# A layernorm, FFT filter and GELU kernel: filter rows loaded without pads, 31 warm-up matmuls, contiguous remainder weights and a new written-out order

## The chip, the cores and the metric

The kernel runs on one core of one Trainium2 chip. The metric is the device time of one execution in microseconds. Before the change the median of three runs is 148.87 us (148.75 to 149.37).

## The reference

The input x is 2048 x 640 in bf16. It is normalized over its 640 columns. Two branches read the result xn: a Fourier filter (two-dimensional real FFT, multiplication by the complex weights w_r + i w_i of 2048 x 321, inverse FFT) and a two-layer network with a GELU (640 to 1536 to 640). The output is x plus both.

```python
def _A_ref(x, w_r, w_i):
    B, S, D = x.shape
    X = jnp.fft.rfft2(x.astype(jnp.float32), axes=(-2, -1))
    X = X * (w_r + 1j * w_i)
    return jnp.fft.irfft2(X, s=(S, D), axes=(-2, -1)).astype(jnp.bfloat16)

def _B_ref(x, w1, b1, w2, b2):
    h = _gelu(jnp.einsum("bsd,df->bsf", x, w1) + b1)
    return jnp.einsum("bsf,fd->bsd", h, w2) + b2

xn = _layernorm(x, axis=-1)
return x + _A_ref(xn, w_r, w_i) + _B_ref(xn, w1, b1, w2, b2)
```

## The kernel before

The 2048 rows lie on 128 partitions, 16 chunks (numbered 0 to 15) of 640 columns each. The work goes through these stages.

- **Normalization (VectorE).** Each chunk has two batch-norm statistics (L480), their aggregation (L482), a reciprocal root (L490 and L491, the latter on GpSimd) and the scaling (L510), which writes xn. Sums and differences of mirrored columns (L540, L544) prepare the Fourier branch.
- **Transposes.** Layer 1 needs xn transposed (xnT). For chunks 0 to 3 TensorE does it (L528, copies at L394 and L395); for chunks 4 to 15 a DMA transpose issued by SyncE (L519).
- **Layer 1 (TensorE, all matmuls at L383).** Blocks of chunks 0-1, 2-3, 4-7, 8-11 and 12-15, each with 12 tiles of 128 hidden features (L575 to L584 for the first, L605 for the others). Five matmuls make one tile; ScalarE applies the GELU (L593, L611). A block needs the transposes of all its chunks. The order on TensorE is: block 0-1, block 2-3, part of layer 2, most of block 8-11, block 4-7, block 12-15.
- **Fourier branch.** Matmuls with the table gtab (L550), evacuated into XV (L556); groups of two or three chunks with the table etab (L635, "bps"); 32x32 matmuls with mtab (L653, "cps", evacuated into Y at L660); the filter itself on VectorE, two multiplications per pair (L678) that read Y and the filter weights Wf, and a sum and a difference (L682); 32x32 matmuls with ntab (L687, "dps"), evacuated into U; DMA transposes of U back into XV (L703); groups of two or three chunks with the table getab (L726, "eps"), evacuated into yo (L730), and sums of mirrored columns (L734, L739).
- **Layer 2 and the end.** Layer 2 (L761) is summed with the last matmul of the Fourier branch (table htab, L777) in PSUM; VectorE adds the bias or what was kept (L780) and writes the result, which a DMA adds onto x in the output (L787, GpSimd) or writes (L784, SyncE). Before that, GpSimd copies x into the output in four transfers (L563), after all filter weights have landed.

A group of matmuls with etab or getab (the functions `width` and `five`, L615 to L623) has four matmuls per chunk over 128 rows and four over 32 rows, the remainders. The stationary operand comes from XV: with etab 128 neighbouring columns, with getab 128 columns 16 elements apart.

The filter weights Wf lie as 32 rows per partition, real and imaginary rows in turn, each padded from 321 to KP = 322 elements; the pads are set to zero at L407, and every filter load waits for that. Partitions with even numbers hold rising rows of the weights, those with odd numbers falling ones. `load_w` (L448) loads 16 rows for 16 partitions at a time: nine loads for w_r, nine for w_i, all on SyncE's queue, one semaphore for all (group "W").

TensorE begins with 39 + 8 matmuls on zeros (`idle`, L409 to L413, WARM at L293). Then the bias of layer 1 is turned into a column by 12 small matmuls (L464).

The order of the work on each engine is written out by hand in ORDER (L253): each word is the number of an operation, a letter for its engine (s SyncE, p TensorE, a ScalarE, d VectorE, g GpSimd) and the PSUM or buffer slots. `arrange` puts the operations into that order, `sync` finds the waits. The numbers that `load`, `mm_us` and the like give as costs served only to find the order; they do nothing in the kernel. Each engine works its list in order, and SyncE issues its DMAs in the order of its list.

Of the kernel before, what the change touches and what calls it, by code (L numbers as in the profile page):

```python
# [9 lines left out]
ACT = mybir.ActivationFunctionType  # L10
# [78 lines left out]
def mm_us(n):  # L89
    return max(n / 2400.0 + 0.0027, 0.0265)  # L90
# [6 lines left out]
def act_us(n, ptr=0):  # L97
    return 0.067 + n / 1200.0 + 0.078 * ptr
# [155 lines left out]
9s 2a 0d 4g 6g 125p:1 3g 11a 10s 8p:6 12s 13s 14s 15s 55d 54d 16s 1d 17s 56d 60d 57a 18s 58a 59d 121d:1 19s 61d 124p:1 20s 122p:0 52p:7 62d 21s 123d 126a 63d 64g 22s 279p:0 249p:6  # L254
53a 289p:2 269p:1 23s 239p:5 259p:3 240p 127d 250p 24s 280p 270p 290p 133d:0 260p 25s 128p:4 130p:7 281p 129d 26s 251p 131a 132d 291p 261p 242p 252p 27s 241p 272p 68d 292p 271p 28s
243p 282p 69d 283p 253p 29s 262p 65d 244p 273p 274p 30s 284p 66d 254p 255p 70d 263p 67d 293p 245p 71d 134d:1 264p 72g 285p 135d 275p 137d 276p 256p 141d:0 278a 294p 246p 286p 144d
258a 142p:4 136d 248a 145p:7 143d 265p 247a 295p 146d 287a 266p 296p 148d:0 257a 305p:5 77d 288a 311p:7 147d 268a 323p:4 306p 85d 267a 314p:6 307a 312p 89d 315p 277a 332p:5 93d
297a 324p 92d 320p:3 298a 302p:0 101d 313a 321p 325a 100d 333p 326p:7 322a 152d:0 94d 308p:4 90d 316a 327p 151d 138p:1 91d 328a 139p 97d 309p 334a 95d 317p:6 98d 96g 140a 329p:7
102d 99d 330p 103d 149d 299p:5 5g 104g 184d:0 318p 331a 303p 150d 300p 182d 319a 7g 154p:1 81d 304a 153p 183s 197d:1 573p:6 301a 195d 310a 574p 186d:0 155a 196s 590p:4 187d 84d
575p 74d 591p 76d 198s 82d 576p 73d 592p 191d:1 185s 78d 189d 577p 188d 190d 578p 75d 83d 200d:0 31s 593p 79d 199d 32s 80g 192p:1 86d 594p 579d 33s 193p 113d 595p 34s 87d 203d:1  # L260
88g 374p:6 35s 204d 156d:1 375p 596d 157s 386p:0 376a 116d 377p:4 158d 194a 201d 159s 404p:7 114d 171d:0 398p:5 202d 115d 169d 36s 405p 161d:0 206p:1 172s 108d 406a 205p 117d 387p
207a 109d 389p:7 160d 170s 401p:6 118d 164d:1 388a 119d 165d 378p 120g 106d 37s 402p 163d 110d 379a 162d 390p 38s 221d:1 403a 399p 105d 39s 166p:0 223d 400a 167p 107d 356p:4 224s
111d 225d:0 391a 112g 226d 357p 359p:7 227d:1 358a 40s 229d 347p:5 228d 168a 230d 222s 173d:0 348p 174d 360p 210d:0 41s 231p:0 177d:0 361a 335p:6 208d 42s 349a 178d 232p 175d 336p
211s 176d 234a 212d:0 344p:7 213d 337a 180p:3 215d:1 209s 179p 216d 233a 345p 214d 350p:6 217d 181d 346a 43s 218p:0 219p 44s 365p:7 220a 45s 351p 338p:4 46s 352a 446p:0,0 47s 48s
366p 448d 447a 49s 339p 428p:5 50s 51s 443p:0,1 429p 445a 444d 410p:6 340a 733d 411p 367a 461p:0 434p:4 462a:1 463d:0 435p 430a 464p:0 436a 416p:5 235g 465d 466a 417p 412a 236g
471d:0 449p:0,1 418a 472d 237g 425p:7 450a 468d:1 238g 422p:4 467d 451a 426p 423p 469d:0 353p:5 473d:1 424a 470d 485p:0 427a 431p:4 487d:1 486a:0 432p 474d 626p:6 433a 478p:0
380p:4 480d:0 479a:2 381p 475p:0 382a 354p 477d 476a 419p:4 355a 484s 420p 488p:0 413p:5 490a 489d 483s 414p 421a 495d:1 455p:0,0 415a 481s 496d 392p:4 457a 456d 482s 383p:5 492d:0
393p 384p 394a 491d 452p:0,1 385a 498d:0 494d:1 368p:4 453a 454d 369p 341p:5 370a 497d 493d 512p:0 371p:4 513a:1 514d:0 372p 499p:0 373a 342p 500d:2 501a:0 362p:4 343a 363p 509p:0
395p:5 511d 510a 396p 515d:1 502p:0 627p 503a 504d 628p 364a 520d:0 505s 458p:0,1 397a 519d 629p 459a 507s 460d 609p:4 610p 516d 506s 536p:0 521d:0 630p 538a:0 518d:1 611p 517d
508s 537a:1 522d 631p 533p:0 612p 535a 534d 613p 632d 526p:0 614p 543d:0 527a:1 662p:6 540d:1 528a:2 663p 544d 523p:0 664p 615d 524a 665p 546d:1 525a 530s 645p:4 539d 666p 545d  # L270
667p 529s 541d:0 542d 646p 668d 647p 531s 547p:0 698p:6 548d:0 532s 699p 549d:1 700p 648p 550p:0 701p 551a 552d 702p 554s 703p 649p 704d 650p 556s 440p:7 651d 441p 553s 437p:4 442a
407p:5 555s 408p 564p:6 565p 438p 566p 557p:0 567p 558d:1 559a 568p 439a 560d:0 569p 409a 561d 583p:0 562d:0 563d 681p:4 585a:0 584d 570p 682p 571d:7 619p:0 586d:0 572g 587d 683p
620a:1 589d:1 684p 621a 588d 685p 686p 655p:0 687d 622d:0 600p:6 657a:0 743d 601p 623d 656a 602p 636p:4 580p:0 616p:2 581d:6 637p 638p 617d:2 639p 625d:0 618g 603p 624d 640p 658d:0
652p:2 604p 653d:0 641p 654g 605p 606p 642p 607d:3 691p:0 643d:5 608g 672p:6 659d 693a:1 644g 673p 692a 633p:4 674p 660d:0 675p 634d:7 676p 661d 635g 726p:0 695d:0 708p:4 582g
727a:0 694d 677p 728a 709p 678p 597p:0 679d:2 669p:2 710p 598d:0 680g 711p 688p:6 670d:7 712p 599g 697d:1 713p 696d 734p:0 689d:4 717p:2 714p 718p 690g 715d:5 719p 729d:0 671g 735p
730d 753p:7 720p 716g 705p:4 736p 706d:2 737p 732d:0 707g 721p 731d 722p 723p 738p 724d:1 739p 725g 744p:4 745p 746p 740p 747p 741d:7 754p 755p 748p 756p 749p 742s 750p 757p 762p:6
751d:0 758p 759p 763p 764p 760d 752s 765p 766p 767p 761s 768p 769d 770s
# [15 lines left out]
WARM = (39, 8)  # L293
# [3 lines left out]
def bass_parallel_sum__spectral_gfnet__dense_activation_gelu__prompt_kernel(  # L297
# [21 lines left out]
    with ExitStack() as es:  # L319
# [93 lines left out]
        idle(WARM[0], 0.1067 * 32 + (WARM[0] - 32) * mm_us(128))  # L413

# [18 lines left out]
        for j, at in enumerate((5.92, 6.93, 7.9, 9.75, 10.7)):  # L433
            if j == 3:
                load_x(2, 2, next(pr), at=8.75)
            load(W1[:, F * j:F * j + F], w1v[:, j, :], B_w1s[j], 393216, prio=next(pr), at=at)
        load(gtab[:], const["G"], B_g, 524288, prio=next(pr), at=12.0)
        for c, at in zip(range(4, 16, 2), (13.2, 14.7, 15.5, 16.3, 17.1, 17.9)):
            load_x(c, 2, next(pr), at=at)
# [8 lines left out]
        def load_w(wsrc, p0, off, row, n, step):  # L448
            w_ops.append(load(bass.AP(tensor=Wf, offset=p0 * WP + off, ap=[[2 * WP, 16], [2 * KP, n], [1, 321]]),
                 bass.AP(tensor=wsrc.tensor, offset=wsrc.offset + row * 321, ap=[[128 * 321, 16], [step * 321, n], [1, 321]]),  # L450
                 B_w, 16 * 642 * n, after=[wpad], rate=150e3, issue=0.645, group="W", prio=next(pr)))
        for ri, wsrc in enumerate((A_w_r, A_w_i)):
            for half in range(4):
                p0, off = 32 * half, ri * KP
                load_w(wsrc, p0, off, 16 * half, 16, 1)
                if half:
                    load_w(wsrc, p0 + 1, off, 128 - 16 * half, 16, -1)
                else:
                    load_w(wsrc, p0 + 1, off, 64, 1, 1)
                    load_w(wsrc, p0 + 1, off + 2 * KP, 127, 15, -1)  # L460
# [3 lines left out]
        pe([("128", 0.7)], 200, lambda: [(psb(B_b1ps.slot, [[1, 1]], fc), part(gT, 0, 1, 512 * (fc // 4) + fc % 4, [[4, 128]]), ident[0:1, 0:1], True, True)  # L464
# [30 lines left out]
        for pair in range(8):  # L495
# [10 lines left out]
            for n in range(2):  # L506
# [15 lines left out]
                for j0, j1, engs in ((0, 2, ["dve"]), (2, 5, ["act"])) if c < 2 else ((0, 5, ["dve", "act"]),):  # L522
# [7 lines left out]
                    tp = K.op([("pe", nj * mm_us(128))], pr, xt, reads=[B_xn, xn, B_id], writes=[tps], segs=[("128", nj * mm_us(128))])  # L530
                    if j0 and not c:
                        idle(WARM[1], WARM[1] * mm_us(128), gate=[tp])
# [113 lines left out]
        for P in range(4):  # L646
# [20 lines left out]
            def wv(pair, r):  # L667
                return view(Wf, (16 * (pair % 2) + 4 * (pair // 2) + r) * KP, [[2 * KP, 2], [0, 2], [1, KP]])
# [53 lines left out]
        for gi, (c0, n) in enumerate(GROUPS):  # L722
# [3 lines left out]
            pe(five_segs(n, 0.045), pr, lambda c0=c0, n=n, eps_=eps_: five(  # L726
                eps_.slot, n, lambda i, g, p0, k: part(XV, p0, k, 2048 * g + c0 + i, [[16, 128]]), getab),
                reads=B_v + [B_ge], writes=[eps_], gate=[fin_ops[c0 - 5]] if c0 > 8 else [])
# [92 lines left out]
```

## Time and profile before

| | before |
|---|---|
| median of 3 runs | 148.87 us |
| the profiled execution | 149.58 us |
| its span, first to last instruction | 147.8 us |
| TensorE busy | 141.9 us (96%) |
| VectorE busy | 110.0 us (74%) |
| ScalarE busy | 72.3 us (49%) |
| multiplications by the filter, L678 | 16 of 822 ns |
| DMA transposes of xnT (L519), issue to landing | 2.5 / 3.6 / 5.0 us (least, median, most) |
| filter loads, issued between | 28.6 and 51.5 us |

The page lists per engine the busy time, then the span in 40 slices, the DMA queues, the chain of work that ended last (followed back from the last instruction to what released each step), the costliest groups of instructions, and the DMAs. "L383 PE MATMUL ps<-xnT,W" is a matmul of line 383 that writes the tile ps from xnT and W1; "<-" behind an idle time names what ended it. "SPq" is SyncE's queue, where a DMA is issued; "PEld" is TensorE's loading of weights. Matmul records can be missing.

### The profile page before, as it was taken

How to read it: one execution, taken by the hardware profiler on the slowest of the kernel's cores; microseconds unless marked ns; L12 is line 12 of the kernel's file. 1: busy time of each engine (PE TensorE's matmuls, PEld its weight loads, DVE VectorE, ACT ScalarE, POOL GpSimd, SP SyncE). 2: the span in 40 equal slices, each digit the busy share in tenths (PEclk: the TensorE clock that was granted, in tenths of full speed). 3: DMA queues.
4: the chain of work that ended last, by engine and by line, in shares of the span. 5: the costliest groups of instructions: out<-in, count | busy, mean ns of one | idle time of the engine just before them, and what ended most of it. 6: DMA issues, size and time to landing. Idle time of an engine off the chain costs nothing.

```text
span 147.8 us, 3951 instructions
## 1 busy us (share of the span) xinstructions
PE 141.9 (96%) x1677; PEld 90.5 (61%) x1692; DVE 110.0 (74%) x240; ACT 72.3 (49%) x118; POOL 21.5 (15%) x35
## 2 busy tenths in 40 slices
PE   7999999999799999999999999999999999999993
PEld 7999995655456645445644545555666656655573
DVE  2688999999996367856966979864099787769543
ACT  3615995047598579977775756121075400430000
POOL 1002040301200005000000000000002024545620
DMA  5999999569999998988700670475302107777974
GB/s 119 305 402 399 378 388 132 113 141 135 165 163 160 158 161 218 350 334 45 141 4 0 41 138 10 89 93 106 71 4 24 20 4 84 93 89 91 114 87 114
DMA packets 29843, 21.01 MB, mean 142 GB/s; under 512 B 20225, under 2 KB 27137, under 8 KB 29826
## 3 DMA queue, kind: packets, MB, share of 16 engines
q1 hardware_dynamic: 27232, 15.84, 49.7%
q0 software_dynamic: 2592, 4.92, 17.8%
q8 instruction: 13, 0.21, 0.6%
q14 instruction: 4, 0.03, 0.1%
q10 hardware_dynamic: 2, 0.00, 0.0%
HBM read 13.54 MB, written 5.24 MB: 127 GB/s over the span
## 4 chain that ended last, share of the span: by engine, by line
PE 89%; DVE 5%; DMA 2%; issue 2%; SPq 1%
PE ps L383 88%; DMA xnT<-T 2%; DVE W L780 1%; DVE stats L480 1%; PE ps L528 1%; DVE T L544 1%; DVE T L510 1%; DVE T L540 1%; DVE X L771 1%; SPq L519 1%; DVE mv L482 0%; DVE warm L399 0%; DVE ve L490 0%
## 5 line engine op out<-in xcount | busy, mean ns | idle before, releaser
L383 PE MATMUL ps<-xnT,W 128*128 128x512 bf16 (+2 forms) x336 | 56.9, 320 | 1.0 <-DMA xnT<-T 1.0
L383 PE MATMUL ps<-W,gT 128*128 128x128 bf16 (+3 forms) x382 | 55.0, 292 | 1.5 <-issue 1.0
L383 PEld LDWEIGHTS ps<-W,gT 128*128 128x128 bf16 x396 | 30.1, 98 | 22.5 <-issue 1.7
L383 PEld LDWEIGHTS ps<-xnT,W 128*128 128x128 bf16 x336 | 31.4, 114 | 18.5 <-ACT gT L611 2.8
L611 ACT ACTIVATE gT<-ps,b1col 128x512 bf16<-128x512 f32 (+1 forms) x48 | 28.4, 638 | 15.1 <-PE ps L383 15.1
L787 POOL DMA_DIRECT2D out_dram<-W x14 | 12.3, 990 | 71.0 <-DVE W L780 71.0
L394 ACT ACTIVATE Wf<-ps 128x960 bf16<-128x960 f32 (+1 forms) x10 | 8.5, 888 | 17.9 <-PE ps L383 17.9
L480 DVE BATCH_NORM_STATS2 stats<-X 128x6 f32<-128x320 bf16 x32 | 14.0, 477 | 2.1 <-DMA X<-in_A_x_dram 2.1
L678 DVE TENSOR_TENSOR T<-Y,Wf 128x1288 bf16<-128x1288 bf16 x16 | 12.5, 822 | 0.0
L491 POOL TENSOR_TENSOR rstd<-ve,mhalf 128x2 f32<-128x2 f32 (+1 forms) x8 | 6.0, 744 | 31.9 <-DVE ve L490 31.8
L395 DVE CAST Y<-ps 128x644 bf16<-128x644 f32 x7 | 5.8, 829 | 5.4 <-PE ps L383 5.4
L394 ACT ACTIVATE Xb<-ps 128x960 bf16<-128x960 f32 (+1 forms) x7 | 8.0, 1166 | 3.4 <-PE ps L383 3.3
L544 DVE TENSOR_TENSOR T<-T 128x512 bf16<-128x512 bf16 (+1 forms) x32 | 9.0, 313 | 0.2
L394 ACT ACTIVATE XV<-ps 128x1280 bf16<-128x1280 f32 (+2 forms) x8 | 8.9, 1109 | 0.5 <-PE ps L383 0.5
L395 DVE CAST Xb<-ps 128x960 bf16<-128x960 f32 (+1 forms) x5 | 5.5, 1105 | 4.2 <-PE ps L383 4.2
L394 ACT ACTIVATE Y<-ps 128x644 bf16<-128x644 f32 x9 | 6.3, 708 | 4.1 <-PE ps L383 4.0
L510 DVE TENSOR_SCALAR T<-X,mv,rstd 128x640 bf16<-128x640 bf16 x16 | 6.9, 441 | 1.5 <-POOL rstd L491 1.0
L383 PE MATMUL ps<-getab,XV 32*128 32x160 bf16 (+1 forms) x128 | 7.5, 242 | 0.0
L540 DVE TENSOR_TENSOR T<-T 128x640 bf16<-128x640 bf16 x16 | 7.4, 480 | 0.1
L739 DVE TENSOR_TENSOR Wf<-Wf 128x960 bf16<-128x960 bf16 (+1 forms) x12 | 6.7, 596 | 0.9 <-PE ps L383 0.8
L780 DVE TENSOR_TENSOR W<-ps,b2bc 128x640 bf16<-128x640 f32 x6 | 4.8, 821 | 3.3 <-PE ps L383 3.3
L383 PE MATMUL ps<-etab,XV 32*128 32x160 bf16 (+1 forms) x128 | 7.2, 232 | 0.0
(53 smaller groups left out, 123.1 us busy)
## 6 DMA issues: line engine op xcount, KB each, us to landing
out_dram<-in_A_x_dram POOLq DMA_DIRECT2D x4, 640.0 KB, 7.3
X<-in_A_x_dram SPq DMA_DIRECT2D x7, 320.0 KB, 9.4
out_dram<-W POOLq DMA_DIRECT2D x14, 160.0 KB, 3.4
W<-in_B_w_dram SPq DMA_DIRECT2D x5, 384.0 KB, 5.8
W<-in_B_w_dram SPq DMA_DIRECT2D x3, 640.0 KB, 12.8
Wf<-in_A_w_r_dram SPq DMA_DIRECT2D x7, 160.5 KB, 3.9
Wf<-in_A_w_i_dram SPq DMA_DIRECT2D x7, 160.5 KB, 4.6
gtab<-c_G SPq DMA_DIRECT2D x1, 512.0 KB, 9.1
```

The source lines that it names most:

```text
L383: ins = e.matmul(o_, lhsT=lw, rhs=rh, start=st, stop=sp_, skip_group_check=True)
L394: return e.activation(dst(), src(), ACT.Copy, scale=scale)
L395: return e.tensor_copy(dst(), src())
L480: st_ops.append(K.op([("dve", 0.393)], pr, lambda e, _, c=c, h=h: e.bn_stats(stats[:, c, 6 * h:6 * h + 6], view(X, c * D + H2 * h, [[1, H2 ...
L510: o = K.op([("dve", 0.356)], pr, lambda e, _, c=c, n=n, xnv=xnv: e.tensor_scalar(out=xnv(n, 0, [[1, D]]), in0=view(X, c * D, [[1, D]]), sc ...
L540: K.op([("dve", 0.39)], pr, lambda e, _, k=k, op=op, xnv=xnv, x1v=x1v: e.tensor_tensor(out=x1v(H2 * k, [[D, 2], [1, H2]]), in0=xnv(0, 0, [ ...
L544: ring_ops.append(K.op([("dve", 0.333 if w == 128 else 0.136)], pr, lambda e, _, op=op, x1v=x1v, xfv=xfv, o_=o_, o0=o0, o1=o1, w=w: e.tens ...
L611: K.op([("act", act_us(128 * nt, 1) + 0.02)], pr + PRIO["gelu"], lambda e, _, c0=c0, nt=nt, fc=fc, hps=hps: e.activation(gT[:, fc, 128 * c ...
L678: filt_ops.append(K.op([("dve", 0.738)], pr, lambda e, _, k=k, Y=Y, TB=TB, pair=pair: e.tensor_tensor(out=view(TT, TB.slot * 8 * KP + k * ...
L739: K.op([("dve", 0.068 + n / 6)], pr + 3, lambda e, _, k=k, op=op, y2=y2, yf=yf, n=n: e.tensor_tensor(out=view(Wf, YF + yf.slot * 3 * D + ( ...
L780: K.op([("dve", dve_us(w))], 95, lambda e, _, os_=os_, fps=fps, o0=o0, w=w, xo=xo, base=base: e.tensor_tensor(out=view(W1, OST + os_.slot ...
L787: last.append(K.op([("pool", 0.9)], 450, lambda e, _, c=c, os_=os_: e.dma_start(ov[:, c, :], view(W1, OST + os_.slot * D, [[1, D]]), accum ...
```

## The change

1. **Filter without pads.** Wf holds 16 real rows and then 16 imaginary rows per partition, 321 elements each, with no pads; the memset covers one element behind the last row. The multiplications read 322 elements per row from rows 321 apart, the last of them the first of the next row (it meets a zero of Y).
2. **Fewer filter loads.** The rising rows of all 64 even partitions come in one load for w_r and one for w_i, each partition one piece of 16 x 321 elements. The falling rows stay in loads of 16 partitions. 12 loads instead of 18.
3. **Warm-up.** 31 matmuls on zeros instead of 39 + 8; the 12 bias matmuls now come right behind them, ahead of the first transposes.
4. **Remainder copies.** For the last four groups with getab ScalarE copies the remainder's part of XV into contiguous columns of the buffer T, and the remainder matmuls read their stationary operand from there. The first two groups stay as they were.
5. **A new ORDER** for all engines.

```diff
-WARM = (39, 8)
+WARM = 31
...
-        wpad = K.op([("pool", 0.2)], 447, lambda e, _: e.memset(view(Wf, KP - 1, [[KP, 32], [1, 1]]), 0.0), writes=[B_wpad])
+        wpad = K.op([("pool", 0.2)], 447, lambda e, _: e.memset(view(Wf, 32 * 321, [[1, 1]]), 0.0), writes=[B_wpad])
...
+            dst, src, more = [[321, n], [1, 321]], [[step * 321, n], [1, 321]], dict(rate=155e3, issue=0.645)
+            if step > 0:
+                dst, src, more = [[1, 321 * n]], [[1, 321 * n]], dict(rate=350e3, issue=0.5)
+            if quarters > 1:
+                dst, src = [[2 * WP, 16 * quarters]] + dst, [[16 * 321, quarters], [128 * 321, 16]] + src
+            else:
+                dst, src = [[2 * WP, 16]] + dst, [[128 * 321, 16]] + src
...
+            off = ri * 16 * 321
+            load_w(wsrc, 0, off, 0, 16, 1, 4)
+            for half in range(1, 4):
+                load_w(wsrc, 32 * half + 1, off, 128 - 16 * half, 16, -1)
+            load_w(wsrc, 1, off, 64, 1, 1)
+            load_w(wsrc, 1, off + 321, 127, 15, -1)
...
-                return view(Wf, (16 * (pair % 2) + 4 * (pair // 2) + r) * KP, [[2 * KP, 2], [0, 2], [1, KP]])
+                return view(Wf, (16 * r + 8 * (pair % 2) + 2 * (pair // 2)) * 321, [[321, 2], [0, 2], [1, KP]])
...
+            if gi > 1:
+                K.op([("act", act_us(128 * n) + 0.18 * n)], pr + 5, lambda e, _, c0=c0, n=n: e.activation(
+                    view(TT, 128 * c0, [[128, n], [1, 128]]), view(XV, 4 * 2048 + c0, [[1, n], [16, 128]]), ACT.Copy), reads=B_v, writes=[B_xr], after=filt_ops)
...
+                eps_.slot, n, lambda i, g, p0, k: part(TT, p0, k, 128 * (c0 + i), [[1, 128]]) if gi > 1 and g == 4 else part(XV, p0, k, 2048 * g + c0 + i, [[16, 128]]), getab),
+                reads=B_v + [B_ge, B_xr], writes=[eps_], gate=[fin_ops[c0 - 5]] if c0 > 8 else [])
```

What the new ORDER does on SyncE's queue, written with names (T4 is the transpose of chunk 4, Wr and Wi loads of real and imaginary weights):

```
before: ... w2 w2 w2 etab mtab T8 T10 T11 T9 ntab Wr Wr Wr Wr T4 T5 Wr T7 T6 Wr Wr Wr T15 Wr T14 Wi Wi T13 T12 Wi Wi Wi Wi Wi Wi Wi getab htab ...
after:  ... w2 w2 w2 T9 T10 T11 T8 etab mtab ntab Wr(rising) T4 T5 T7 T6 Wr Wr Wr Wr Wr Wi(rising) Wi Wi Wi Wi T15 T13 T12 T14 Wi getab htab ...
```

On TensorE the stages keep their sequence; within them the tiles are arranged anew. On ScalarE the four remainder copies stand around the copies of the second group with getab (yo): the first ahead of it, the other three behind it and ahead of the third group's.

More of the change, by code (lines that the diff above doesn't have):

```diff
@@ L412, in idle @@
             return pe([("128", us)], 300, lambda: [(psb(b.slot, [[1, 128]]), warm[:], warm[:], True, True) for _ in range(n)], reads=[B_warm], writes=[b], **kw)
-        idle(WARM[0], 0.1067 * 32 + (WARM[0] - 32) * mm_us(128))
+        idle(WARM, WARM * mm_us(128))
         B_b1t, B_b2b = Buf("b1t"), Buf("b2")
@@ L432, in bass_parallel_sum__spectral_gfnet__dense_activation_gelu__prompt_kernel @@
         load(part(gT, 0, 1, 0, [[1, F]]), b1v, B_b1t, 3072, q="act", prio=409, at=3.2)
-        for j, at in enumerate((5.92, 6.93, 7.9, 9.75, 10.7)):
+        for j, at in enumerate((6.05, 7.05, 8.0, 9.85, 10.8)):
             if j == 3:
-                load_x(2, 2, next(pr), at=8.75)
+                load_x(2, 2, next(pr), at=8.85)
             load(W1[:, F * j:F * j + F], w1v[:, j, :], B_w1s[j], 393216, prio=next(pr), at=at)
-        load(gtab[:], const["G"], B_g, 524288, prio=next(pr), at=12.0)
-        for c, at in zip(range(4, 16, 2), (13.2, 14.7, 15.5, 16.3, 17.1, 17.9)):
+        load(gtab[:], const["G"], B_g, 524288, prio=next(pr), at=12.3)
+        for c, at in zip(range(4, 16, 2), (13.7, 14.9, 15.7, 16.55, 17.35, 18.15)):
             load_x(c, 2, next(pr), at=at)
@@ L446, in bass_parallel_sum__spectral_gfnet__dense_activation_gelu__prompt_kernel, with load_w @@
         WP = 32 * KP
[L448 to L451, printed above, removed]
-        for ri, wsrc in enumerate((A_w_r, A_w_i)):
[L453 to L460, printed above, removed]
+        def load_w(wsrc, p0, off, row, n, step, quarters=1):
+            dst, src, more = [[321, n], [1, 321]], [[step * 321, n], [1, 321]], dict(rate=155e3, issue=0.645)
[5 more added lines that the diff above has]
+                dst, src = [[2 * WP, 16]] + dst, [[128 * 321, 16]] + src
+            w_ops.append(load(bass.AP(tensor=Wf, offset=p0 * WP + off, ap=dst), bass.AP(tensor=wsrc.tensor, offset=wsrc.offset + row * 321, ap=src),
+                 B_w, 16 * 642 * n * quarters, group="W", prio=next(pr), **more))
+        for ri, wsrc in enumerate((A_w_r, A_w_i)):
+            off = ri * 16 * 321
[4 more added lines that the diff above has]
+            load_w(wsrc, 1, off + 321, 127, 15, -1)
         load(getab[:], const["GE"], B_ge, 204800, prio=next(pr))
@@ L529, in xt @@
                         return ins
-                    tp = K.op([("pe", nj * mm_us(128))], pr, xt, reads=[B_xn, xn, B_id], writes=[tps], segs=[("128", nj * mm_us(128))])
-                    if j0 and not c:
-                        idle(WARM[1], WARM[1] * mm_us(128), gate=[tp])
+                    tp = K.op([("pe", nj * mm_us(128))], pr, xt, reads=[B_xn, xn, B_id], writes=[tps], hard=[b1op], segs=[("128", nj * mm_us(128))])
                     us = {"dve": 0.06 + 0.068 * nj, "act": act_us(128 * nj)}
@@ L725, in bass_parallel_sum__spectral_gfnet__dense_activation_gelu__prompt_kernel @@
             eps_ = Buf(f"eps{gi}", psum, 4, ZONE["eps"])
-            pe(five_segs(n, 0.045), pr, lambda c0=c0, n=n, eps_=eps_: five(
-                eps_.slot, n, lambda i, g, p0, k: part(XV, p0, k, 2048 * g + c0 + i, [[16, 128]]), getab),
-                reads=B_v + [B_ge], writes=[eps_], gate=[fin_ops[c0 - 5]] if c0 > 8 else [])
+            B_xr = Buf(f"xr{gi}")
+            if gi > 1:
+                K.op([("act", act_us(128 * n) + 0.18 * n)], pr + 5, lambda e, _, c0=c0, n=n: e.activation(
+                    view(TT, 128 * c0, [[128, n], [1, 128]]), view(XV, 4 * 2048 + c0, [[1, n], [16, 128]]), ACT.Copy), reads=B_v, writes=[B_xr], after=filt_ops)
+            pe(five_segs(n, 0 if gi > 1 else 0.052 * (n - 1)), pr, lambda c0=c0, n=n, eps_=eps_, gi=gi: five(
+                eps_.slot, n, lambda i, g, p0, k: part(TT, p0, k, 128 * (c0 + i), [[1, 128]]) if gi > 1 and g == 4 else part(XV, p0, k, 2048 * g + c0 + i, [[16, 128]]), getab),
+                reads=B_v + [B_ge, B_xr], writes=[eps_], gate=[fin_ops[c0 - 5]] if c0 > 8 else [])
             for v in range(2):
```

50 lines of the change are left out of this document (25 added, 25 removed).

## The prediction

> **What bounds the kernel now.** I read the table of cores first: one core, span 147.8 us, granted clock 1.000. The profiled execution took 149.58 us, 0.5% above the median of 148.87 us; I make the sum on the profiled one and carry the microseconds over to the median. Then the page: TensorE is busy 96% of the span.
>
> ```profile
> PE 141.9 (96%) x1677; PEld 90.5 (61%) x1692; DVE 110.0 (74%) x240; ACT 72.3 (49%) x118; POOL 21.5 (15%) x35
> GB/s 119 305 402 399 378 388 132 113 141 135 165 163 160 158 161 218 350 334 45 141 4 0 41 138 10 89 93 106 71 4 24 20 4 84 93 89 91 114 87 114
> q10 hardware_dynamic: 2, 0.00, 0.0%
> ```
>
> The GB/s row gives an engine's pace: about 400 GB/s over 16 engines while the first loads run, 25 GB/s each. The q10 row (packets, MB, share) is the bias load, all in two packets.
>
> Third, the chain of work that ended last. It is TensorE from end to end, but for one stretch around 39 us:
>
> ```profile
> 35.64 0.80 SPq L519
> 36.44 0.04 issue
> 36.48 2.64 DMA xnT<-T
> 39.12 0.09 issue
> 39.21 23.83 PE ps L383 x268
> ```
>
> TensorE waits there for the last of four DMA transposes. In the list of waits this is its only long wait for a transfer:
>
> ```profile
> PE ps L383 <- DMA xnT<-T: 1.0, 1, 1.0
> POOL out_dram L375 <- DMA Wf<-in_A_w_i_dram: 17.5, 1, 17.5
> ```
>
> Some gaps of 0.16 us behind the remainder matmuls ("issue") precede a 128-wide piece whose 512-wide partner is missing from the trace, so they are no idle time. A gain can come only from that 1.0 us, from the head, and from work that TensorE no longer does. Fourth, SyncE's own timeline, which is one queue in order:
>
> ```profile
> 27.98 0.58 SPq L375 DMA_DIRECT2D ntab<-c_N  x1
> 28.60 2.68 SPq L375 DMA_DIRECT2D Wf<-in_A_w_r_dram  x4
> 31.33 2.61 SPq L519 DMA_TRANSPOSE xnT<-T  x2
> 33.98 0.59 SPq L375 DMA_DIRECT2D Wf<-in_A_w_r_dram  x1
> 34.62 3.15 SPq L519 DMA_TRANSPOSE xnT<-T  x2
> ```
>
> Four filter loads stand ahead of the transposes of chunks 4 and 5. By the semaphore records of the trace the fourth landed at 34.4 us and chunk 4's transpose, issued at 31.3, only at 36.4; chunk 6's, issued with nothing ahead, landed 2.6 us after its issue. So transposes queue behind the loads that were issued before them.
>
> **The change part by part.**
>
> *Head.* 47 warm-up matmuls become 31. They run 0.107 us apart until 6.4 us (then 0.056), so 16 fewer are 1.7 us of TensorE. But the first normalized chunk is ready only at 5.17 us (VectorE, L510), the first W1 slab lands at 6.5 us and the second at 7.5 by the records. Layer 1 starts at 6.6 instead of 7.13, waits for the second slab at 7.5, and is some 0.3 us ahead afterwards. That does not last: block 8-11 starts at 29.41 us, right behind its transposes, the last of which landed at 29.2. VectorE starts 1.2 us earlier (the normalization of chunk 1 no longer waits behind a copy), but then waits for chunk 4, which lands at 14.5 us. Head: 0, between -0.3 and +0.3. If the step in the spacing, which came 5.5 us after the first matmul, counts anew from the pause that now follows 4.3 us, it comes at 9.8: 30 matmuls at 0.107 instead of 0.056 us lose 1.5 us, of which waiting and the head start cover 0.5. That is 1.0 us at most.
>
> *Pads.* The memset (0.24 us, POOL) is off the path. The multiplies at L678 now read rows of 321 elements, of which every second one starts at an odd element. They take 0.822 us for 1288 elements, and L682 takes 0.487 for 644, so an element costs 0.52 ns; at half that pace a multiply would take 0.67 us more, 16 of them 10.7 us of VectorE. The nearest rows are L734 and L739, which read or write from odd starts downwards and still take 0.65 us for 960 elements. I take no cost; both ends go into a rival. [...]
>
> *Filter loads.* 18 become 12. Six issues of 0.61 us less on SyncE are 3.7 us of its time, and the last filter load, which landed at 56.8 us, 0.3 us before the first multiply at 57.1, would be earlier. The rising rows of all four quarters, 64 partitions of 10,272 bytes, 657 KB, become one load, whose source counts 4 x 16 rows of partitions. How many engines carry it decides the case. On 16 at 25 GB/s it moves in 1.6 us, on 4 in 6.6 us, each engine a quarter. Rows: every filter load of before posts 16 landing marks and its outermost count is 16; the bias load, whose outer count is 1, posts two marks and went out in two packets of q10. So the count of engines follows the outermost count; that of the new load's source is 4. I take 4 engines, 6.6 us. [...]
>
> *New order on SyncE.* Now: transposes 9, 10, 11, 8; etab, mtab, ntab; the rising real load; transposes 4, 5, 7, 6; four falling real loads of 16 or 15 rows and one of one row; the rising imaginary load; three falling ones and one row; transposes 15, 13, 12, 14. The first four end at about 27.2 us (27.93 before; the first took 2.2 us against 1.3 for the others, with the two table loads in the queue ahead, which now follow). Three tables and the load take 2.5 us to issue, so the rising load is issued at 29.1 and moves from 30.1 us, one microsecond later, as the first filter load of before did (issued 28.6, landed 31.7, of which 1.1 moving). On the four engines that carry it, the queue then reads:
> - rising real load to 36.7 us;
> - four transposes at 0.7 us (36.37 to 37.05 before) to 39.5, the last landing at 40.1. Block 4-7 starts at 40.2 instead of 39.21: +1.0 us. VectorE's normalization of chunks 7 and 6 waits for them too, but TensorE needs its result only later;
> - falling real loads: an engine's share of one takes some 1.1 us (the last six landed 0.8 to 1.2 us apart, each spread over all engines), four make 4.3 us, to 43.8;
> - rising imaginary load to 50.4; three falling ones to 53.7; four transposes to 56.5, landing at 57.1.
>
> TensorE gets from the start of block 4-7 to block 12-15 in seven tiles of 1.08, six of 0.28, 1.24 + 1.08 + 0.65 + 0.90 = 13.1 us: at 53.3 us. It waits 3.8 us more. Between the two blocks and afterwards it is dense as before. Behind the waiting matmul stand all later matmuls, so the whole +4.8 us stays. With 16 engines the transposes 4 to 7 are limited by their issue (four at 1.3 us from 29.8, landing by 36.5), and TensorE, which gets there at 38.2 us, waits for nothing: -1.0 us.
>
> *Remainder copies.* A group of three chunks takes 1.30 us from getab (strided) against 1.24 from etab (plain), one of two 0.96 against 0.90. At most 0.06 us each, four groups: -0.2 us, between -0.24 and 0. The four copies cost ScalarE 0.5 to 1.0 us each (128x384 took 0.49, the strided 128x960 of Xb 1.27); it waits 17.9 us for TensorE in that stretch. Three of them stand ahead of the copies of the third group, which the fourth group's matmuls wait for: TensorE has 3.0 us of other work there, the queue needs 2.8. Without that cover up to 1 us.
>
> **Sum:** 0 + 4.8 - 0.2 = +4.6 us: 154.2 us on the profiled execution, 153.5 us on the median. Faster engines (a tenth) take 1.2 us off; waits that reach the multiplies or a clock that falls in a 3.8 us idle add up to 3. Own range 150 to 156.5 us.
>
> **Rivals.**
> 1. *The rising loads run on all 16 engines* (the other side: not slower). The place is transposes 4 to 7, the price the 1.0 us of today's wait; it decides if they land before 38.2 us. Then -1.0 - 0.2 = -1.2 us, 147.7 us. For it: the other loads use 16. With a late clock step (31 warm-ups end at 4.3 us, the step came at 6.5), TensorE arrives 1.0 us later and only 0.2 us are left: 148.7 us.
> 2. *Odd rows halve the multiplies.* VectorE idles some 8 us between 57 and 98 us, mostly waiting for TensorE within the same chain, so 2.7 to 10.7 us of the 10.7 show; with 16 engines some +5, 154 us. Against it: L734 and L739.
> 3. *The change doesn't do what it says:* the loads take 6.6 us but the engines work past them, so that the transposes are late by under 1 us: 148.9 us.
>
> **How the numbers follow.** Forecast 0.64; rival 1 fast 0.18, late clock 0.08; rival 2 0.06; rival 3 0.04. More than 0.64 the rows don't bear: none of them shows a load with an outermost count between 1 and 16. Within 0.5% (0.7 us) is about what a measurement of this kernel can't tell from no change. Faster 0.18, same 0.12, slower 0.70. The range 147.5 to 156.3 us takes in rival 1 and leaves out some 2 in 10, the ends of each case.
>
> **What would show it.** Four landing marks on the rising loads instead of 16; TensorE's wait for xnT transposes near 5 us in two places (about 38 to 40 and 53 to 57 us) instead of 1.0; L678 at 0.82 us; eps groups at 1.24 us. Wrong if transposes 4 to 7 land by 38 us, or if L678 takes 1.4 us.

## The result and the profile after

The changed kernel takes **163.34 us** (median of 4 runs, 162.6 to 164.03) against 149.0 us before (148.75 to 149.37): 1.096 times the time, 95% interval 1.0905 to 1.1014. The forecast was 153.5 us, the range 147.5 to 156.3. The direction was right, the size was not: +14.3 us instead of +4.5. The profiled execution took 164.03 us, its span is 162.2 us (147.8 before). Medians below are over all executions of a kernel, while ratios leave out those more than 1.5% above its fastest, so the two can differ by some tenths of a per cent.

First the page of the changed kernel: TensorE's busy time, and the clock that it was granted in 40 slices of 4.05 us.

```profile
PE 146.4 (90%) x1676; PEld 88.8 (55%) x1676; DVE 111.9 (69%) x240; ACT 74.7 (46%) x122; POOL 21.2 (13%) x35
PE   7799999993099972999999999999999999999993
PEclk9999999999659996599999999999999999999999
```

TensorE has two holes (slices 10 and 11, and 16), and late in each the clock drops to half (from 41.83 and from 62.31 us by the clock records). Before, TensorE's row has only a 7 in slice 11 (its slices are 3.7 us long), and the granted clock was 1.000:

```profile
PE   7999999999799999999999999999999999999993
```

The list of waits names them (VectorE has one as well), and the chain of work that ended last shows what stands in them:

```profile
PE ps L383 <- DMA xnT<-T: 10.7, 2, 6.8
DVE T L514 <- DMA xnT<-T: 7.4, 1, 7.4
```

```profile
35.74 1.26 SPq L523
37.00 0.04 issue
37.04 3.37 SPq L523
40.41 0.04 issue
40.45 4.18 DMA xnT<-T
44.64 0.09 issue
44.73 12.49 PE ps L383 x89
57.22 0.02 issue
57.24 1.28 DVE Xb L395
58.52 0.84 SPq L523
59.36 0.04 issue
59.40 1.53 SPq L523
60.94 0.04 issue
60.98 2.70 DMA xnT<-T
63.68 0.09 issue
63.77 28.42 PE ps L383 x413
```

Both holes end with a DMA transpose of xnT: block 4-7 starts at 44.73 us (39.21 before, 40.2 forecast), block 12-15 at 63.77 (57.2 forecast). SyncE's timeline shows the queue:

```profile
29.47 0.74 SPq L375 DMA_DIRECT2D Wf<-in_A_w_r_dram  x1
30.26 11.47 SPq L523 DMA_TRANSPOSE xnT<-T  x4
41.78 3.58 SPq L375 DMA_DIRECT2D Wf<-in_A_w_r_dram  x5
45.40 3.19 SPq L375 DMA_DIRECT2D Wf<-in_A_w_i_dram  x5
48.63 13.62 SPq L523 DMA_TRANSPOSE xnT<-T  x4
```

Four transposes took 5.2 us to issue behind loads on 16 engines (kernel rising_16 below); here 11.5 and 13.6. The packets of the rising loads are the only ones of 10,272 bytes, so the trace shows when they moved: the real one from 31.20 to 40.16 us (9.0 us), the imaginary one from 47.52 to 58.71 (11.2 us). The filter's semaphore got 170 landing marks: 10 falling loads by 16, and 5 for each rising load, one at once and four when it had landed. The multiplications by the filter are what they were:

```profile
L680 DVE TENSOR_TENSOR T<-Y,Wf 128x1288 bf16<-128x1288 bf16 x16 | 12.7, 822 | 0.1
```

### The profile page after: what moved, and what is told of

Same layout as the page of the kernel before. It is cut to its first block, busy times and chain, and to the rows that moved or that the text cites. A ratio compares the mean times of both kernels' runs of the same rounds, so it can differ in the third digit from the quotient of the medians.

```text
span 162.2 us, 3944 instructions
## 1 busy us (share of the span) xinstructions
PE 146.4 (90%) x1676; PEld 88.8 (55%) x1676; DVE 111.9 (69%) x240; ACT 74.7 (46%) x122; POOL 21.2 (13%) x35
## 3 DMA queue, kind: packets, MB, share of 16 engines
q1 hardware_dynamic: 25192, 15.84, 51.9%
## 4 chain that ended last, share of the span: by engine, by line
PE 62%; DVE 16%; DMA 12%; SPq 7%; issue 1%; DVEq 0%
PE ps L383 62%; DMA xnT<-T 6%; DVE stats L484 5%; SPq L523 4%; DMA W<-in_B_w_dram 4%; DMA XV<-U 3%; DVE T L546 2%; SPq L705 2%; DVE T L514 2%; DVE T L542 1%; SPq L375 1%; DVE T L680 1%; DVE X L777 1%; DVE Xb L395 1%; DVE mv L486 1%
## 5 line engine op out<-in xcount | busy, mean ns | idle before, releaser
L383 PE MATMUL ps<-xnT,W 128*128 128x512 bf16 (+2 forms) x336 | 61.9, 334 | 11.5 <-DMA xnT<-T 10.7
L383 PE MATMUL ps<-W,gT 128*128 128x512 bf16 (+3 forms) x396 | 57.6, 295 | 0.2 <-DVE X L777 0.2
L383 PEld LDWEIGHTS ps<-xnT,W 128*128 128x128 bf16 x336 | 31.9, 116 | 31.8 <-issue 17.5
L383 PEld LDWEIGHTS ps<-W,gT 128*128 128x128 bf16 x396 | 30.1, 98 | 23.2 <-issue 1.2
L613 ACT ACTIVATE gT<-ps,b1col 128x512 bf16<-128x512 f32 (+1 forms) x48 | 28.5, 634 | 26.6 <-PE ps L383 26.2
L484 DVE BATCH_NORM_STATS2 stats<-X 128x6 f32<-128x320 bf16 x32 | 14.3, 477 | 2.3 <-DMA X<-in_A_x_dram 2.1
L680 DVE TENSOR_TENSOR T<-Y,Wf 128x1288 bf16<-128x1288 bf16 x16 | 12.7, 822 | 0.1
L394 ACT ACTIVATE Wf<-ps 128x960 bf16<-128x960 f32 (+1 forms) x8 | 6.7, 868 | 11.8 <-DVE W L786 7.0
L394 ACT ACTIVATE XV<-ps 128x1280 bf16<-128x1280 f32 (+1 forms) x7 | 8.2, 1178 | 5.4 <-PE ps L383 5.4
L546 DVE TENSOR_TENSOR T<-T 128x128 bf16<-128x128 bf16 (+1 forms) x32 | 9.0, 314 | 0.5 <-PE ps L383 0.4
L777 DVE TENSOR_TENSOR X<-ps,b2bc 128x640 f32<-128x640 f32 x7 | 5.7, 820 | 2.6 <-PE ps L383 2.4
L395 DVE CAST Wf<-ps 128x960 bf16<-128x960 f32 (+1 forms) x4 | 4.3, 1074 | 4.6 <-PE ps L383 4.5
L383 PE MATMUL ps<-Wf,htab 128*128 128x512 bf16 (+3 forms) x33 | 7.3, 295 | 0.0
```

The costliest lines, as they stand in the source:

```text
L383: ins = e.matmul(o_, lhsT=lw, rhs=rh, start=st, stop=sp_, skip_group_check=True)
L394: return e.activation(dst(), src(), ACT.Copy, scale=scale)
L395: return e.tensor_copy(dst(), src())
L484: st_ops.append(K.op([("dve", 0.393)], pr, lambda e, _, c=c, h=h: e.bn_stats(stats[:, c, 6 * h:6 * h + 6], view(X, c * D + H2 * h, [[1, H2 ...
L546: ring_ops.append(K.op([("dve", 0.333 if w == 128 else 0.136)], pr, lambda e, _, op=op, x1v=x1v, xfv=xfv, o_=o_, o0=o0, o1=o1, w=w: e.tens ...
L613: K.op([("act", act_us(128 * nt, 1) + 0.02)], pr + PRIO["gelu"], lambda e, _, c0=c0, nt=nt, fc=fc, hps=hps: e.activation(gT[:, fc, 128 * c ...
```

## The experiments

**Theory.** The rising loads run on four engines, the transposes behind them on those engines wait, and the clock that falls in the holes costs more. **Rivals.** The new order costs the time by itself; the loads are slow for another reason than their engines; the shorter warm-up costs it. Each kernel ran beside the kernel before on its chip; ratios are against that one. A new order is shown with names, as above, and not as it stands in the code.

**rising_16: the engines alone.** Four loads of 16 partitions in place of each rising load, at the same place.

```diff
-            load_w(wsrc, 0, off, 0, 16, 1, 4)
+            load_w(wsrc, 0, off, 0, 16, 1)
+            for half in range(1, 4):
+                load_w(wsrc, 32 * half, off, 16 * half, 16, 1)
```

> Each rising load of 64 partitions is cut into four of 16 partitions (pieces of 16 x 321 elements as before), at the same place of SyncE's queue; nothing else changes. Theory (four engines carry the rising load, and the transposes behind it wait for them): the loads move on 16 engines in well under 2 us each, TensorE's two waits for xnT (6.8 and 3.9 us) fall to 1 us or less together, the clock stays at full speed, and the time is 147.5 to 149.5 us, 14 to 16 us below the changed kernel. Rival (the new order, the shorter warm-up or the copies cost the time): the waits stay or come back elsewhere, over 155 us. Rival (the loads are slow because of their long pieces, not because of their engines): each still takes over 4 us and the first wait stays above 2 us.

151.43 us, ratio 1.017 (1.0125 to 1.0209): 11.9 us of the 14.3 are gone, with the same order. The same 64 packets of 10,272 bytes now move in 3.0 us. The wait left is

```profile
PE ps L383 <- DMA xnT<-T: 1.8, 1, 1.8
```

The theory's main step holds; its number, 149.5 us at most, was missed, so something else costs 2 us.

**halves: what sets the number of engines.** The rising loads in two pieces of two quarters each (`quarters=2`).

> The changed kernel with each rising load cut into two of 32 partitions: the outermost count of the source is 2 instead of 4. Theory (the number of engines follows that count): each load runs on two engines, three marks per load (two and one for the rest), 6.2 us or more for each; if both take the same two engines, 12.4 us or more for the pair, and TensorE's first wait grows from 6.8 to 9 us or more, time 165 to 172 us. Rival (a load of 642 KB is spread over four engines for another reason, such as its size or its 64 partitions): the loads of half the size take four engines or more, about 3 us each, and the time is that of the changed kernel or less.

172.81 us, one execution. 172 landing marks are 160 and three for each of the four loads: two engines each. The two real ones moved one behind the other, 31.11 to 40.40 and 40.12 to 46.85 us.

```profile
PE ps L383 <- DMA xnT<-T: 20.6, 2, 11.3
```

The number of marks went with the outermost count of the source: at 16, 4 and 2 a load posted 16, 4 and 2 (the last two with one more at once). That a mark stands for an engine is my reading, and the times fit with it: 32 packets of 386 ns, the least in the changed kernel, are 6.2 us on two engines (6.7 and 9.3 here), and 64 on four are the same (7.5 in rise_last below). The two halves in a row fit with the same engines; which engines these were no record names.

**late: the queue.** The rising loads stay on four engines but stand behind the transposes.

```diff
-SyncE: Wr(rising) T4 T5 T7 T6 Wr x5 Wi(rising) Wi x4 T15 T13 T12 T14 Wi
+SyncE: T4 T5 T7 T6 Wr(rising) Wr x5 T15 T13 T12 T14 Wi(rising) Wi x5
```

> The changed kernel with its two rising loads as they are (four engines each), but on SyncE's queue the real one stands behind the transposes of chunks 4 to 7 and the imaginary one, with the falling imaginary ones, behind those of chunks 12 to 15. Theory (it is the queueing of the transposes behind the load, not the load itself, that stops TensorE): the load still takes 9 to 11 us, TensorE's waits for xnT fall from 10.7 to at most 2 us, and what is late next is the first multiplication with the filter, some 4 to 6 us, of which a part reaches TensorE: 149 to 155 us. Rival (the transposes are slow in this order for another reason): the waits for xnT stay above 5 us and the time above 157 us.

165.04 us, ratio 1.107 (1.1038 to 1.1107). TensorE's wait for transposes fell from 10.7 to 2.3 us, as expected, but the time did not: the loads took 12.0 and 13.8 us, and the first multiplication waited 13 us for the last of them.

```profile
DVE T L680 <- DMA Wf<-in_A_w_i_dram: 13.0, 1, 13.0
ACT Y L394 <- DVE T L680: 10.6, 1, 10.6
PE ps L383 <- DMA xnT<-T: 2.3, 1, 2.3
```

The transposes do queue behind the load; my 4 to 6 us for what comes next was too small. Four engines have too much to move before the filter begins, whether the loads stand ahead of the transposes or behind them.

**act_queue: another queue.** ScalarE issues the two rising loads (`q="act"`).

> The changed kernel with the two rising loads issued by ScalarE on its own queue, in the same places of the order; their shape stays. Theory A (the queue's order holds the transposes back: one queue works in order on each engine): the transposes no longer stand behind the load, TensorE waits for xnT under 3 us in all, 149 to 153 us. Theory B (the four engines themselves are the limit, whatever the queue): each transpose has a share on those engines and waits for 10 KB packets between its own; waits of 4 us or more stay, 155 to 163 us. Both have four landing marks for the load.

164.58 us, ratio 1.100 (1.0948 to 1.106): theory B, 1.6 us above its range. The real load moved from 30.8 to 40.2 us and the imaginary one, which ScalarE issued already at 37.8 us, from 41.8 to 50.7 (47.5 to 58.7 in the changed kernel). Two of the transposes 4 to 7 landed behind the first load, at 41.3 and 41.9 us, and two only behind the second, at 51.2 and 51.9, so TensorE waited long once instead of twice:

```profile
PE ps L383 <- DMA xnT<-T: 12.6, 1, 12.6
```

A second queue did not help here: 164.58 us against 163.34, with 12.6 us of waiting for transposes against 10.7.

**rise_last: the size of the load.** The rising imaginary load behind everything else on the queue.

> The changed kernel with the rising imaginary load behind all other loads and transposes of the first part (behind htab) on SyncE's queue, where nothing else moves beside it. It measures that load by itself. Theory (four engines at 386 ns per piece of 10,272 bytes when alone, shared with transposes and falling loads in the changed kernel): 16 pieces per engine, 6.2 to 6.8 us from the first packet to the last, against 9 to 11 us there. Rival (the load is slow by itself, say because its pieces start at odd addresses): 9 us or more here too. The first multiplication waits for it, so the time is no matter.

One execution, 159.85 us. The load moved from 57.83 to 65.29 us, 7.5 us, beside the end of the loads ahead of it; the median packet took 387 ns, 16 of which are 6.2 us. In the changed kernel the packets took 484 ns (real) and 661 ns (imaginary) on average, at least 386. So 6.2 to 6.6 us is the load alone (an estimate from these packets), and the rest is what moves beside it.

**loads_only: parts 1 and 2 in the old order**, with the old warm-up and no copies.

> The kernel before with parts 1 and 2 of the change alone: filter rows without pads and one rising load of 64 partitions for each of real and imaginary weights, in the place of the first rising load of each; old order, 39 + 8 warm-ups, no remainder copies. Theory (the two loads on four engines are what costs): TensorE waits some 5 to 8 us for transposes 4 to 7 and 2 to 5 us for 12 to 15, the clock falls behind both, 159 to 165 us. Rival (the loads cost this much only in the new order, which puts all four transposes behind them): under 156 us.

159.21 us, ratio 1.065 (1.0612 to 1.069): the loads alone cost some 10 us even where the old order spreads the transposes among them.

```profile
PE ps L383 <- DMA xnT<-T: 9.4, 2, 7.4
```

**fill, fill_second, fill_long: the clock.** Matmuls on zeros put into TensorE's holes.

```diff
+TensorE, ahead of block 4-7: idle(100) in fill and fill_long
+TensorE, ahead of block 12-15: idle(60) in fill, idle(64) in fill_second, idle(105) in fill_long
```

> The changed kernel with 100 matmuls on zeros (128x128) put on TensorE ahead of block 4-7 and 60 ahead of block 12-15, where it stands idle for 6.8 and 4.1 us; the loads and the queue stay. Theory (the granted clock falls to half after these idle times, and matmuls 427 instead of 216 ns apart for 3.8 and some 5 us cost 1.9 and 2.5 us): the matmuls on zeros fit into the idle times, the clock stays at 1.00, the waits end when they did, and the time falls by 3.5 to 4.5 us to about 159.3 us. Rival (the clock follows something else than TensorE's own idling, or the lost time is made up later anyway): less than 1 us.

> The changed kernel with 64 matmuls on zeros ahead of block 12-15 only (3.6 us, its idle time there is 3.9 us). In kernel fill the 100 ahead of block 4-7 kept the clock at full speed and the time did not fall, and the 60 ended 3.8 us too early, since the last transposes landed 1.9 us later than in the changed kernel. Theory (the transposes of chunks 12 to 15 land when the DMA queue lets them, so TensorE's speed between the two waits is worth nothing, and the half clock behind the second wait is worth 2.0 to 2.5 us): the clock stays up behind the second wait and the time is 160.5 to 161.5 us. Rival (the multiplications or VectorE set the end and the half clock is hidden): 163 us or more.

> Kernel fill with 105 instead of 60 matmuls on zeros ahead of block 12-15. Theory (the half clock behind the second wait costs 2 to 2.9 us: from the start of block 12-15 to the end of the span it is 98.4 us in the changed kernel, 98.2 in fill and 97.7 in fill_second, whose clock fell, and 95.6 to 95.8 in warm_47 and rising_16, whose clock did not): the idle time left is under 2 us, the clock stays up, that stretch takes 95.5 to 96.5 us, and the time is 160 to 162.5 us by when the transposes land. Rival (that stretch is longer because VectorE is behind, not because of the clock): it stays above 97.5 us.

Medians 164.57, 163.0 and 163.24 us, ratios 1.107 (1.1034 to 1.1098), 1.085 (1.079 to 1.0916) and 1.094 (1.0875 to 1.0997). All three miss the times expected. In the first two the matmuls on zeros ended 3.6 and 2.4 us too early and the clock fell again. In fill_long it stayed up. Windows (length, busy time and count of TensorE first; the third last column is the granted clock) behind the second hole, the changed kernel and then fill_long:

```profile
64.00:68.00 4.00, 4.00 (x41) 1.14 (x40) 0.83 (x1) 1.39 (x2) 2.06 (x4) 0.50 0.94 238
68.00:72.00 4.00, 4.00 (x65) 1.92 (x64) 2.34 (x4) 2.48 (x5) 0.23 (x1) 0.86 0.95 356
```

```profile
64.00:68.00 4.00, 3.01 (x61) 1.21 (x58) 0.83 (x1) 1.28 (x2) 1.71 (x3) 1.00 0.99 256
68.00:72.00 4.00, 4.00 (x68) 2.26 (x68) 3.41 (x5) 3.55 (x5) 0.58 (x2) 1.00 0.96 334
```

From the start of block 12-15 to the end of the span fill_long took 95.7 us instead of 98.4: the half clock there is worth 2.7 us. The records give the same: half clock from 62.31 to 69.14 us, of which TensorE worked 5.4, half of that lost. But the median is that of the changed kernel: in these profiles the last transposes landed 0.6 to 2.0 us later (64.2 to 65.6 against 63.68 us). Why is open; it may be scatter of executions.

**before_31 and combined_31: the warm-up.** 31 warm-ups in the kernel before (`WARM = (30, 1)`) and in the kernel combined (below).

> The kernel before with 30 + 1 warm-up matmuls instead of 39 + 8, nothing else. In kernels late, fill and act_queue (31 warm-ups) the spacing went from 107 to 55 ns only at 8.7 to 10.1 us, in the kernel before at 6.4. Theory (fewer warm-ups bring the slow spacing into layer 1): 0.3 to 1.2 us slower than before, 149.1 to 150.0 us. Rival (layer 1 is held by the slabs of W1 and the last normalized chunks in any case): within 0.3 us of before.

> Kernel combined with 31 warm-ups instead of 47. Theory (31 warm-ups cost what they cost in the kernel before, 0.7 to 1.7 us, because TensorE pauses ahead of layer 1 and in some executions runs it at the slow spacing): 149.8 to 150.8 us, with a wider scatter than combined's 148.1 to 149.65. Rival (before_31 lost it through one late transpose, which this order hides): within 0.4 us of combined's 149.0.

150.69 us (148.81 to 152.04), ratio 1.008 (1.0052 to 1.0108), and 149.95 us (148.7 to 151.05), ratio 1.007 (1.0039 to 1.0107): 1.0 to 1.2 us in either order, with a wide scatter. The first lies above the 149.1 to 150.0 expected. Their own profiled executions happen not to show a late step to full speed: that of combined_31 is its fastest execution, and in that of before_31 TensorE waited 2.1 us ahead of block 4-7 (1.0 before), where a transpose landed at 39.9 us. Other kernels with 31 show the late step. Windows at the head of the kernel before and of sync_order (the count behind TensorE's busy time is the thing):

```profile
7.00:8.00 1.00, 1.00 (x23) 0.99 (x20) 0.31 (x3) 0.22 (x2) 0.57 (x1) 1.00 0.90 338
8.00:9.00 1.00, 1.00 (x21) 1.00 (x20) 0.93 (x3) 0.02 (x1) 0.00 (x0) 1.00 1.03 392
```

```profile
7.00:8.00 1.00, 1.00 (x12) 1.00 (x11) 0.16 (x1) 0.00 (x0) 0.00 (x0) 1.00 1.02 370
8.00:9.00 1.00, 1.00 (x13) 1.00 (x11) 0.30 (x2) 0.00 (x0) 0.00 (x0) 1.00 1.03 400
```

TensorE is "busy" in both, with half as many matmuls. By their starts, the 128-wide matmuls of layer 1 include 17 to 25 that are 107 ns apart in 9 of 12 profiles with 31 warm-ups, and at most one in the six with 47; its 64th matmul starts at 11.3 to 13.0 us in the nine, at 10.3 to 11.4 in the others. That this step is what the two medians lost fits in size, but no profile of these two kernels shows it.

**warm_47, sync_order, combined: the rest of rising_16's loss.** 47 warm-ups; the transposes of 12 to 15 ahead of the falling imaginary loads; both, and those of 4 to 7 ahead of two of the four rising real loads.

```diff
-SyncE: Wr(rising) x4 T4 T5 T7 T6 Wr x5 Wi(rising) x4 Wi x4 T15 T13 T12 T14 Wi
+SyncE: Wr(rising) x2 T4 T5 T7 T6 Wr(rising) x2 Wr x5 Wi(rising) x4 T15 T13 T12 T14 Wi x5
```

> Kernel rising_16 (four loads of 16 partitions in place of each rising load) with 47 warm-up matmuls in one group instead of 31. In the profile of rising_16 TensorE stands still for 0.48, 0.80 and 1.30 us before 8.24 us, and its matmuls then run 107 instead of 55 ns apart until 11.96 us, about 1.7 us lost. Theory (31 warm-ups leave pauses from which the slow spacing starts anew): with 47 the spacing stays at 55 ns behind the warm-ups and the time falls by 0.8 to 1.7 us, to 149.7 to 150.6. Rival (layer 1 waits for the slabs of W1 anyway, the warm-ups only fill): within 0.5 us of rising_16's 151.4.

> Kernel rising_16 with one thing moved on SyncE's queue: the transposes of chunks 15, 13, 12 and 14 stand ahead of the falling imaginary loads instead of behind four of them. Theory (what is left of the loss with 16 engines is mostly TensorE's wait of 2.04 us ahead of block 12-15, which comes from the place of these transposes in the new order): the wait goes, 149.3 to 150.0 us. Rival (the multiplications wait for the last filter load, which lands at 57.5 us either way, and the end hangs on them): at most 0.7 us of it is kept, 150.7 us or more.

> Kernel rising_16 with 47 warm-ups, the transposes of chunks 12 to 15 ahead of the falling imaginary loads, and those of chunks 4 to 7 ahead of two of the four rising real loads. The profile of warm_47 shows three idle times of TensorE that are left: 0.60 at 7.44 us (W1), 1.04 at 39.51 and 0.92 at 53.40 (transposes). Theory (these are what keeps it above the kernel before): the last two go, 148.0 to 149.0 us. Rival (the rest of the new order, in the filter stage, costs as much): 149.5 us or more.

150.79 us, ratio 1.011 (1.0068 to 1.0148); 150.77 us, ratio 1.014 (1.0096 to 1.0179); combined 149.0 us, ratio 0.999 (0.9969 to 1.0011). Each of the first two alone leaves most of rising_16's loss and lies in the other's interval; warm_47 missed its 149.7 to 150.6 narrowly, sync_order its 149.3 to 150.0. Together, and with the transposes 4 to 7 moved as well, they bring the time back to the kernel before, and not below it.

**no_pads and no_copies: the two parts that were to save.** Part 1 alone in the kernel before; combined without the copies.

> The kernel before with part 1 of the change and nothing else: filter rows of 321 elements without pads, all 18 loads of 16 partitions kept (the rising ones now one piece of 16 x 321 elements per partition), old order, old warm-up. Theory (the layout costs nothing and saves nothing on TensorE): within 0.5 us of before, multiplications at 0.82 us. Rival (longer pieces bring the loads in earlier, so the transposes behind them too): 0.5 to 1.0 us faster.

> Kernel combined without the four remainder copies: all remainder matmuls read XV, as in the kernel before. Theory: the groups with getab go from 1.25 back to 1.30 us (three chunks) and from 0.93 to 0.96, the stage from the first of them to the end from 41.4 to 41.6 us, the time 0.2 us up, which the runs can hardly tell. Rival (contiguous columns make no difference, the new order saved the 0.4 us of that stage): groups the same within 0.01 us.

148.99 us, ratio 1.000 (0.9973 to 1.0035), and 149.04 us against combined's 149.0: no difference that these runs can tell. The profile tells for the copies: the remainder's weight loads, combined first (from the copy) and then no_copies (from XV; the mean mixes in loads of 128 rows, those of 32 rows alone take 148 ns),

```profile
L383 PEld LDWEIGHTS ps<-getab,T 32*128 32x128 bf16 x44 | 0.7, 92 | 0.3
```

```profile
L383 PEld LDWEIGHTS ps<-getab,XV 32*128 32x128 bf16 (+1 forms) x128 | 6.5, 147 | 1.3
```

By the matmuls' starts a group of three chunks takes 1.25 us instead of 1.30, and from the first such group to the end it is 41.4 us in combined, 41.6 in no_copies and 41.8 before: 0.2 us from the copies, 0.2 from the order.

## Why the prediction was wrong

The **mechanism was right**: four engines, transposes that queue behind the load, two waits of TensorE for them (forecast to end at 40.2 and 57.2 us, measured to end at 44.7 and 63.8), no cost of the odd rows. **The terms of the chain were mis-sized.** The step that failed is "four transposes to 56.5, landing at 57.1": the last landed at 63.7 us. Term by term, forecast and measured:

| on the four engines | forecast | measured |
|---|---|---|
| rising real load starts | 30.1 us | 31.2 us |
| rising real load | 6.6 us | 9.0 us |
| to the last landing of transposes 4 to 7 | 3.4 us | 4.5 us |
| falling real loads | 3.7 us | 2.9 us |
| rising imaginary load | 6.6 us | 11.2 us |
| falling ones, to the last landing of 12 to 15 | 6.7 us | 5.0 us |
| last landing | 57.1 us | 63.7 us |

- **The load at its own pace.** 25 GB/s per engine is close to the pace of the fastest packets (386 ns for 10,272 bytes are 26.6 GB/s). I used it as if nothing moved beside it. The loads and transposes overlap and, as the waits of late and act_queue suggest, share these engines: a packet of the imaginary load took 661 ns on average, and that load 4.6 us more than forecast; part of it comes back in the shorter rows below it.
- **SyncE stalls too.** I let the four transposes follow the load at 0.7 us each. The second took SyncE 5.45 us to issue, from 31.55 to 37.00 us, and the third 3.37 (1.28 where nothing is in the way), so that the fourth was issued at 40.45 us, after the load's end, and landed 4.18 us later: 1.1 us more in the first wait. (The chain above begins the second only at 35.74 us, behind an operation of VectorE, but all normalizations that had to come first had ended by 31.63.) What I wrote of VectorE was wrong but harmless: the normalization that waits for these landings, 7.4 us, is that of chunks 14 and 15, not of 7 and 6. It began at 43.56 us, and SyncE came to their transposes only at 48.63.
- **The clock.** It stood in the range, "up to 3", and not in the sum. It cost 2.7 us behind the second wait by the profiles, though the medians of the fill kernels do not show it. Behind the first it fell as well (half from 41.83 to 48.66 us), but there TensorE only came to its second wait 2 us later. With 6.6 us of later transposes and 2.7 of clock the sum of 4.6 becomes 13.9, of 14.4 in the two spans.
- **Head.** "0, between -0.3 and +0.3" failed. The later step that I gave to rival 1 as a special case ("at 9.8", "1.0 us at most") is what mostly happens: full speed at 8.7 to 10.1 us in eight of twelve profiles, 1.0 to 1.2 us. It was tested with loads on 16 engines. In the changed kernel's own profile full speed came at 4.3 us; what the head adds to its median, ahead of the waits for the transposes, was not tried by itself.
- **Rival 1** had its condition wrong and its price too low: 16 engines in this order give 151.4 us and not 147.7 or 148.7, since four of the falling loads stand ahead of transposes 12 to 15 (1.8 us of waiting in rising_16), on top of the head. The gain of 1.0 us at transposes 4 to 7 did not come either: with 47 warm-ups (warm_47) they landed at 39.4 us and not by 36.5.
- **Right:** the remainder copies (-0.2 us by the profiles), L680 at 822 ns, four marks behind the first. No run shows the halving of the multiplications in rival 2, nor the 10.7 us that it was priced with: with every second row from an odd start they take 822 ns, as before.

## What to carry to other kernels

Before merging loads, count the outermost dimension of the source: here the merged load saved three issues of 0.6 us each and, by its marks, gave up 12 of 16 engines (the real one moved for 9.0 us, its packets in rising_16 for 3.0). When a queue's transfers share engines, add up what each engine must move before the deadline, not what each transfer takes alone. And treat an idle time of TensorE as dearer than it looks, since the clock may be at half when the work comes back, as here from 62.31 to 69.14 us (2.7 us by the profiles).

## What the runs showed of the hardware that was not expected

- Half-clock stretches in the clock records last 3.41, 6.83, 10.24 or 13.65 us, multiples of 3.41, where the end of the span does not cut them off. The mean clocks of the profiled executions fit with it: 0.989 over 151.0 us in rising_16, 0.979 over 162.0 in fill_second and 0.968 over 159.4 in loads_only are 3.3, 6.8 and 10.2 us at half clock in sum. Each profile's clock changes all lie on one grid of 3.41 us; in the changed kernel they stand at 4.29, 41.83, 48.66, 62.31 and 69.14 us, 11, 2, 4 and 2 steps apart. There the two windows of this grid ahead of the half clock were idle for 3.41 us (38.42 to 41.83) and 2.46 us (58.90 to 62.31), so one that was only mostly idle was enough. In the profiles together, all 13 windows at full clock in which TensorE stood idle for 1.97 us or more by the matmuls' modelled ends (1.97 in loads_only, 2.15 in fill_second) were followed by half clock, and none with 1.50 us or less was. With 1.8 us it went both ways in rising_16: half from 8.53 to 11.95 us behind three pauses, full behind the pause that ended at 55.22. The length of one pause did not decide: 2.3 us in late, which fell into two windows with 1.50 and 0.76, left the clock alone. Full speed came back only behind windows with under 0.6 us of idle time; in the changed kernel it came behind two with 0.0, while behind those with 2.90 us (41.83 to 45.24) and 1.46 us (62.31 to 65.72) the clock stayed at half.
- The granted clock stands at 1.00 in the windows at the head although matmuls run 107 ns apart there: the clock records of these profiles begin only with the first step to full speed (at 4.29 us in the changed kernel, where the spacing goes from 107 to 56 ns; the profile of the kernel before has none, though its spacing does so at 6.4 us). At the head of these profiles the count of matmuls tells, not the clock column.
